# RWKV attention and a routed expert layer in one kernel: ranks one turn later, halved first products, own rows of three units on GpSimd

## The chip, the cores and the metric

The kernel runs on one core of one Trainium2 chip. A core has five engines with queues of their own: TensorE (PE in the profile, with its weight loads shown apart as PEld), VectorE (DVE), ScalarE (ACT), GpSimd (POOL) and SyncE (SP), which here issues the transfers. [...] The metric is the device time of one launch in microseconds (us), the median of several runs; lower is better. All data are float32.

## The reference

Two layers follow each other. The first is a linear attention with decay, per batch (4), head (8) and step (768), with heads of 48 channels:

```python
for t in range(S):
    kt, vt, rt = (k[:, :, t], v[:, :, t], r[:, :, t])
    cur = np.einsum('bhd,bhe->bhde', u[None] * kt, vt)
    y[:, :, t] = np.einsum('bhd,bhde->bhe', rt, state + cur)
    state = w[None, :, :, None] * state + np.einsum('bhd,bhe->bhde', kt, vt)
```

Its output, turned to 3072 tokens of 384 channels, goes into a router with eight experts. Each token is sent to the expert whose embedding has the largest cosine with it:

```python
logits = xn @ en.T / tau            # xn, en: rows divided by their norms
expert_idx = np.argmax(logits, axis=1)
...                                 # probs: softmax of logits, gate_w: its value at expert_idx
for e in range(E):
    mask = expert_idx == e
    h = np.maximum(x[mask] @ w1[e], 0.0)
    out[mask] = gate_w[mask, None] * (h @ w2[e])
```

## The kernel before

The sequence is cut into 6 chunks of 128 steps, and with 4 batches this makes 24 units; unit i is chunk i // 4 of batch i % 4. Four units of one chunk are a group. Within a chunk the recurrence is written as matrix products: K and R are turned (transposed) and scaled by powers of the decay w, scores are formed and masked, and what the state of earlier chunks contributes is added. The step's own term, which u weighs, is computed apart: `diag` is the sum over channels of K, u and R, and `xd` (the own rows) is V times `diag`.

The decays' powers and unit 0 are prepared like this:

```python
    def busy(columns):
        ps = k.ps.tile([128, 512], F32, name="wake", tag="y")
        nc.tensor.matmul(ps[:, 0:columns], k.ones, wide[:, 0:columns], start=True, stop=True)

    for _ in range(WAKE):
        busy(512)
# ...
    t = pool.tile([128, NP, C], F32, name="wpow")
    for p in range(NP):
        nc.vector.tensor_tensor_scan(
            t[:, p, :], wc[:, p : p + 1].to_broadcast([128, C]), k.ones, 1.0, ALU.mult, ALU.mult
        )
    mid = pool.tile([128, NP], F32, name="mid")
    nc.vector.reciprocal(mid, t[:, :, C // 2])
    kp = k.work.tile([128, NP, C], F32, name="kp", tag="AT0")
    nc.vector.tensor_mul(kp, t[:, :, ::-1], mid[:, :, None].to_broadcast([128, NP, C]))
    k.rpow = pool.tile([128, NP, C], F32, name="rpow")
    for p in range(NP):
        nc.scalar.mul(k.rpow[:, p, :], t[:, p, :], mid[:, p : p + 1])

    kt = turned_k(k, 0)
    k.KT[0] = k.work.tile([128, NP, C], F32, name="KT", tag="KT")
    nc.vector.tensor_mul(k.KT[0], kt, kp)
    turn_r(k, 0)
    ps = k.ps.tile([128, NP, 2, DP], F32, name="kpT", tag="xp")
    for p in range(NP):
        nc.tensor.transpose(ps[:, p].rearrange("q s d -> q (s d)"), kp[:, p, :], k.ident)
    busy(192)
    k.kpow = pool.tile([128, H, D], F32, name="kpow")
    nc.scalar.copy(k.kpow.rearrange("q (p s) d -> q p s d", s=2), ps[:, :, :, 0:D])
    cast(k)
    first = k.Kpad[0].rearrange("q (p s) d -> q p s d", s=2)[:, :, :, 0:D]
    nc.vector.tensor_mul(first, first, ps[:, :, :, 0:D])
```

Own rows exist in two forms, one on ScalarE with four scalings for each half of the heads, one as a single product on GpSimd, which only the last unit uses:

```python
def own_rows(k, i, half):
    if half == 0:
        k.xd[i] = k.work.tile([128, H, D], F32, name="xd", tag="xd")
    diag, V = k.diag[i], k.loaded[i][2]
    for h in range(half * H // 2, (half + 1) * H // 2):
        k.nc.scalar.mul(k.xd[i][:, h, :], V[:, h, :], diag[:, h : h + 1])


def own_rows_once(k, i):
    k.xd[i] = k.work.tile([128, H, D], F32, name="xd", tag="xd")
    k.nc.gpsimd.tensor_mul(k.xd[i], k.loaded[i][2], k.diag[i][:, :, None].to_broadcast([128, H, D]))
```

Each unit's R and K are turned on TensorE into a PSUM tile. The tags name PSUM banks: "tp" has two banks that are used in turn, and `rt`, `yrows`, `lgT` and `rank` all take them; "st" has one.

```python
def turn_r(k, i):

    nc = k.nc
    R = k.loaded[i][1]
    rt = k.ps.tile([128, NP, C], F32, name="rt", tag="tp")
    for p in range(NP):
        nc.tensor.transpose(rt[:, p, :], pair(R, p), k.ident)
    k.RT[i] = k.work.tile([128, NP, C], F32, name="RT", tag="RT")
    nc.vector.tensor_mul(k.RT[i], rt, k.rpow)
# ...
HELD = {"tp": (0, 1), "at": (2, 3), "y": (4, 5), "st": (6,), "xp": (7,), "ps": (0, 1, 6, 7, 2, 3, 4, 5)}
```

The rows of a unit are turned back and added to the own rows; squares are summed for the norms; the rank of each token within its expert comes from two small products, and its place is read from them:

```python
def rows(k, i):
    # ...
    y = k.ps.tile([128, 2, NP // 2, 2 * DP], F32, name="yrows", tag="tp")
    # ... four transposes of yT
    nc.vector.tensor_add(
        by_bank(X), y.rearrange("t s q (u d) -> t s (q u) d", d=DP)[:, :, :, 0:D], by_bank(k.xd.pop(i))
    )

def squares(k, g, b):
    sq = k.work.tile([128, DM], F32, name="sq", tag="sq")
    k.nc.scalar.activation(sq, g.X[:, b, :], ACT.Square, accum_out=g.ssq[:, b : b + 1])


def ranks(k, g):

    mm = k.nc.tensor.matmul
    g.rank = k.ps.tile([128, E, B], F32, name="rank", tag="tp")
    mm(g.rank, k.umask, g.oh, start=True, stop=False)
    mm(g.rank, k.ones, g.pre, start=False, stop=True)


def places(k, g):
    nc, p = k.nc, k.rt
    at = p.tile([128, E, B], F32, name="at", tag="at")
    nc.vector.tensor_mul(at, g.rank, g.oh)
    with nc.allow_low_precision(reason="whole numbers, one of each sum's terms not zero"):
        nc.vector.reduce_sum(k.pos[:, g.c, :], at.rearrange("p e b -> p b e"), axis=AX.X)
```

The loop over the units, one turn for each, gives the order in which every engine gets its instructions. `on` calls a step for one unit, `of_group` for a unit's rows, `whole` for a group when its last unit is reached. The steps that matter here, in their order:

```python
SQUARES = {1: (), 2: (), 3: (), 4: (0, 1), 5: (2, 4), 6: (3, 5)}
# ...
for i in range(-1, units):
    # ... load(k, i + AHEAD)
    whole(places, i - 4)
    whole(logits_out, i - 3)
    if i >= 0:
        on(turn_r, i + 1)
    # ...
    if B <= i < units - 1:
        on(own_rows, i, 0)
    if i >= 0:
        on(turn_k, i + 1)
    # ...
    on(scaled, i + 2)          # Kpad: K times powers, GpSimd
    on(own, i + 2)             # KU: K times u, then times R, GpSimd
    for n in SQUARES.get(i, (i - 1,)):
        of_group(squares, n)
    if B <= i < units - 1:
        on(own_rows, i, 1)
    # ... choose and before (VectorE)
    whole(located, i - 4)
    # ... gates, lanes, listed
    on(own_sum, i + 1)         # diag, VectorE
    on(sums, i)                # y: state part, then scores times V; ScalarE copies it to yT
    on(states, i)
    # ... carry
    on(scores, i + 1)
    on(masked, i + 1, 0)
    on(rows, i)
    on(masked, i + 1, 1)
    # ... of_group(put, i)
    of_group(turn_rows, i - 1) # xp
    whole(logits, i - 2)
    whole(ranks, i - 3)
    # ...
    if 3 <= i < 3 + len(k.ring):
        k.nc.gpsimd.memset(k.ring[i - 3], 0.0)
```

After the loop two experts get an early tile, then all eight run, each as products of its tokens with its two weight matrices, and rows are written to their tokens by indirect transfers.

Of the kernel before, what the change touches and what calls it, by code (L numbers as in the profile page):

```python
# [10 lines left out]
F32 = mybir.dt.float32  # L11
I32 = mybir.dt.int32
ACT = mybir.ActivationFunctionType
ALU = mybir.AluOpType
# [3 lines left out]
B, H, S, D = 4, 8, 768, 48  # L18
DM, E, F = H * D, 8, 1024
N = B * S  # L20
C = 128
NCH = S // C
DP = 64
NP = H // 2
# [14 lines left out]
TG = TT // TM  # L39
WAKE = 2  # L40
AHEAD = 5
SQUARES = {1: (), 2: (), 3: (), 4: (0, 1), 5: (2, 4), 6: (3, 5)}


class Net:
# [3 lines left out]
def build_first(k):  # L49


    nc, pool = k.nc, k.aconst
    wc = pool.tile([128, NP], F32, name="wc")
    nc.vector.memset(wc, 1.0)
    with nc.allow_non_contiguous_dma(reason="384 words"):
        for s, q in ((0, nc.sync), (1, nc.scalar)):
            q.dma_start(out=wc[s * DP : s * DP + D, :], in_=k.w.rearrange("(p s) d -> s d p", s=2)[s])
    k.ones = k.const.tile([128, 128], F32, name="ones")
    nc.vector.memset(k.ones, 1.0)
    wide = k.work.tile([128, 512], F32, name="wide", tag="AT1")  # L60
    nc.vector.memset(wide, 1.0)
    k.ident = k.const.tile([128, 128], F32, name="ident")
    make_identity(nc, k.ident)

    def busy(columns):
        ps = k.ps.tile([128, 512], F32, name="wake", tag="y")
        nc.tensor.matmul(ps[:, 0:columns], k.ones, wide[:, 0:columns], start=True, stop=True)

    for _ in range(WAKE):
        busy(512)  # L70
    k.Kpad, k.Rpad = (
        [pool.tile([128, H, DP], F32, name=f"{name}{i}") for i in range(count)]
        for name, count in (("Kpad", 4), ("Rpad", AHEAD + 2))
    )
    pads = k.Kpad + k.Rpad
    for t in pads:
        nc.gpsimd.memset(t[:, :, D:DP], 0.0)
    load(k, 0, k.Kpad[0])
    for i in range(1, AHEAD - 1):
        load(k, i)  # L80
    load_rows(k)


    nc.gpsimd.tensor_scalar(wc, wc, W_MIN, W_MAX, ALU.max, ALU.min)
    build_numbers(k)
    own_k(k, 0)
    t = pool.tile([128, NP, C], F32, name="wpow")
    for p in range(NP):
        nc.vector.tensor_tensor_scan(
            t[:, p, :], wc[:, p : p + 1].to_broadcast([128, C]), k.ones, 1.0, ALU.mult, ALU.mult  # L90
        )
    mid = pool.tile([128, NP], F32, name="mid")
    nc.vector.reciprocal(mid, t[:, :, C // 2])
    kp = k.work.tile([128, NP, C], F32, name="kp", tag="AT0")
    nc.vector.tensor_mul(kp, t[:, :, ::-1], mid[:, :, None].to_broadcast([128, NP, C]))
    k.rpow = pool.tile([128, NP, C], F32, name="rpow")
    for p in range(NP):
        nc.scalar.mul(k.rpow[:, p, :], t[:, p, :], mid[:, p : p + 1])

    kt = turned_k(k, 0)  # L100
    k.KT[0] = k.work.tile([128, NP, C], F32, name="KT", tag="KT")
    nc.vector.tensor_mul(k.KT[0], kt, kp)
    turn_r(k, 0)
    ps = k.ps.tile([128, NP, 2, DP], F32, name="kpT", tag="xp")
    for p in range(NP):
        nc.tensor.transpose(ps[:, p].rearrange("q s d -> q (s d)"), kp[:, p, :], k.ident)
    busy(192)
    k.kpow = pool.tile([128, H, D], F32, name="kpow")
    nc.scalar.copy(k.kpow.rearrange("q (p s) d -> q p s d", s=2), ps[:, :, :, 0:D])
    cast(k)  # L110
    first = k.Kpad[0].rearrange("q (p s) d -> q p s d", s=2)[:, :, :, 0:D]
    nc.vector.tensor_mul(first, first, ps[:, :, :, 0:D])
    k.wC = t[:, :, C - 1 : C].to_broadcast([128, NP, D])
# [16 lines left out]
def load_rows(k):  # L130
    nc = k.nc
    k.emb_rows = k.aconst.tile([E, DM], F32, name="emb")
    nc.sync.dma_start(out=k.emb_rows, in_=k.emb)
    k.tau_rows = k.aconst.tile([E, 1], F32, name="tau")
    nc.sync.dma_start(
        out=k.tau_rows, in_=bass.AP(tensor=k.tau.tensor, offset=k.tau.offset, ap=[[0, E], [1, 1]])
    )
    k.wrow = k.const.tile([1, DM], F32, name="wrow")
    nc.sync.dma_start(out=k.wrow, in_=k.w.rearrange("(o h) d -> o (h d)", o=1))
# [172 lines left out]
def pair(t, p):  # L312
    return t[:, 2 * p : 2 * p + 2, :].rearrange("q h d -> q (h d)")
# [35 lines left out]
def own_rows_once(k, i):  # L349
    k.xd[i] = k.work.tile([128, H, D], F32, name="xd", tag="xd")  # L350
    k.nc.gpsimd.tensor_mul(k.xd[i], k.loaded[i][2], k.diag[i][:, :, None].to_broadcast([128, H, D]))


def turn_r(k, i):

    nc = k.nc
    R = k.loaded[i][1]
    rt = k.ps.tile([128, NP, C], F32, name="rt", tag="tp")
    for p in range(NP):
        nc.tensor.transpose(rt[:, p, :], pair(R, p), k.ident)  # L360
    k.RT[i] = k.work.tile([128, NP, C], F32, name="RT", tag="RT")
    nc.vector.tensor_mul(k.RT[i], rt, k.rpow)  # L362


def turned_k(k, i):
    Kw = k.Kpad[i % len(k.Kpad)]
    kt = k.ps.tile([128, NP, C], F32, name="kt", tag="st")
    for p in range(NP):
        k.nc.tensor.transpose(kt[:, p, :], pair(Kw, p), k.ident)  # L369
    return kt  # L370
# [476 lines left out]
def attention(k):  # L847


    units = B * NCH  # L850

    def on(f, i, *more):
        if 0 <= i < units:
            f(k, i, *more)
# [5 lines left out]
    def whole(f, i, *more):  # L860
        if 0 <= i < units and i % B == B - 1:
            f(k, k.groups[i // B], *more)

    emb, tables = build_experts(k), build_turned(k)
    for i in range(-1, units):
        j = i - SETTLED * B
        if 0 < i + AHEAD < units:
            load(k, i + AHEAD)
        whole(places, i - 4)
        whole(logits_out, i - 3)  # L870
        if i >= 0:
            on(turn_r, i + 1)
        if i == 0:
            own_sum(k, i)
        if B <= i < units - 1:
            on(own_rows, i, 0)
        if i >= 0:
            on(turn_k, i + 1)
        if 0 < i < B:
            own_rows(k, i, 0)  # L880
        whole(turn_logits, i - 3)
        if i == B + 3:
            norms(k, k.groups[0])
        on(scaled, i + 2)
        if i < 0:
            own_r(k, 0)
        on(own, i + 2)
        for n in SQUARES.get(i, (i - 1,)):
            of_group(squares, n)
        if B <= i < units - 1:  # L890
            on(own_rows, i, 1)
        if i > B + 1:
            whole(norms, i - 2)
        if j == 10:
            k.lists = turned_lists(k, perm, "tp")
            lists = taken_by_rank(k, k.lists)
            first = [Early(k, r, *lists, w) for r, w in zip(LAST, k.weights)]
        whole(choose, i - 3)
        whole(before, i - 3)
        whole(located, i - 4)  # L900
        whole(gates, i - 5)
        whole(lanes, i - 5)
        whole(listed, i - 5)
        if 0 <= i < units - 2:
            on(own_sum, i + 1)
        if j == 7:
            load_, count = loads(k, "xp")
        if j == 9:
            expert_of(k, by)
            number = expert_number(k, LAST[0])  # L910
            load_w1(k, number, k.weights[0][0])
        on(sums, i)
        on(states, i)
        for n in (0, 1) if i == 0 else (1,) if 0 < i < B else ():
            own_rows(k, i, n)
        whole(taken, i - 6, "xp")
        whole(exps, i - 4)
        on(carry, i)
        if 0 < i < B + 2:
            next(tables)  # L920
        whole(summed, i - 6)
        if i == B:
            next(emb)
        on(scores, i + 1)
        on(masked, i + 1, 0)
        if i == 0:
            masked(k, i + 1, 1)
        if i == units - 1:
            first[0].turn()
        on(rows, i)  # L930
        if i != 0:
            on(masked, i + 1, 1)
        if i == units - 2:
            own_sum(k, i + 1)
            own_rows_once(k, i + 1)
        of_group(put, i)
        if j == 10:
            load_w2(k, number, k.weights[0][1])
        of_group(turn_rows, i - 1)
        whole(logits, i - 2)  # L940
        whole(ranks, i - 3)
        if i == 0:
            build_constants(k)
        if i in (1, 2, 3):
            next(emb)
        if 3 <= i < 3 + len(k.ring):
            k.nc.gpsimd.memset(k.ring[i - 3], 0.0)
        if j == 8:
            by = order(k, load_)
        if j == 9:  # L950
            settle(k, by, count)
            perm = turner(k, by)
# [29 lines left out]
    load_, _ = loads(k, "xp")  # L982
# [635 lines left out]
```

## Time and profile before

| what | value |
|---|---|
| time, median of 3 runs | 398.76 us (398.46 to 399.27) |
| span of the profiled execution | 396.4 us |
| attention | 0 to about 130 us |
| experts (from the first transposes of gathered rows of the first full block) | 157.5 to 396.4 us |
| ScalarE own-row scalings | 184 of 324 ns (median) |
| VectorE powers of the decay | 4 scans of 128 steps, 3.69 to 5.11 us |

The profile is one execution, recorded by the hardware. Its page gives each engine's busy time, then the span in 40 slices of 9.9 us with the busy share in tenths, then the chain of work that ended last. Rows of instructions give start and duration in us, engine, line of the kernel, operation, the tiles written and read, their shapes, and in brackets the idle time of the engine before them with what ended it. A matmul of float32 appears as several records, and matmuls are pipelined, so the rows of PE overlap; the weight loads (PEld) show gaps more plainly. A wait for several semaphores is put down to the one that came last by the profile, which is not always the right name.

### The profile page before, as it was taken

Reading aid. Unit: us, or ns where it says so; the run is one execution under the profiler, and the core shown is the slowest. Engines: PE = TensorE matmul, PEld = TensorE weight load, DVE = VectorE, ACT = ScalarE, POOL = GpSimd, SP = SyncE. Lnnn points to the kernel's source line nnn. Section 1 sums busy time; section 2 is a strip of 40 time slices with the busy share of each in tenths; the row PEclk is TensorE's granted clock in tenths of the full one; section 3 lists DMA queues with packets and bytes.
Section 4 is the critical chain, followed back from the end, with each engine's and each line's share of the span. In section 5 each row is a group of like instructions: output and inputs, shape, how many; then the busy total and the mean of one; then the engine's idle time right before and its main releaser. Section 6 shows DMA issues by size and latency. Waiting matters only on the chain.

```text
span 396.4 us, 9266 instructions
## 1 busy us (share of the span) xinstructions
PE 386.9 (98%) x3542; PEld 352.5 (89%) x3542; DVE 253.2 (64%) x600; ACT 173.1 (44%) x524; POOL 160.9 (41%) x216
## 2 busy tenths in 40 slices
PE   7999999999999999999999999999999999999993
PEld 4988888889888877899999999999999999799783
DVE  6887878787788670757667668257275456655601
ACT  4887777777677412333333332233323243133120
POOL 7998796858664232500701502220350350200111
PEclk9999999999999999999999999999999999999998
DMA  7899887767606972244705532434164170150111
GB/s 146 163 215 214 189 180 162 157 136 149 142 33 206 288 285 65 87 161 163 255 7 215 196 106 94 133 112 161 55 227 159 43 237 3 40 180 0 41 39 44
DMA packets 93797, 54.35 MB, mean 137 GB/s; under 512 B 76938, under 2 KB 88381, under 8 KB 93747
## 3 DMA queue, kind: packets, MB, share of 16 engines
q1 hardware_dynamic: 90242, 44.26, 41.4%
q0 software_dynamic: 3296, 9.44, 7.3%
q8 instruction: 29, 0.48, 0.5%
q14 instruction: 22, 0.17, 0.1%
q10 hardware_dynamic: 208, 0.00, 0.0%
HBM read 44.45 MB, written 9.63 MB: 136 GB/s over the span
## 4 chain that ended last, share of the span: by engine, by line
PE 86%; SPq 4%; ACT 3%; DMA 2%; DVE 2%; POOL 1%; issue 1%; POOLq 0%; DVEq 0%; ACTq 0%
PE ps L1226 25%; PE ps L1290 18%; PE ps L1330 5%; PE at L388 4%; PE ps L1344 4%; PE y L452 4%; PE early_h L1036 3%; PE early_y L1045 3%; PE ps L1204 3%; PE yrows L470 2%; PE ps L1174 2%; PE y L443 2%; PE rt L360 2%; PE kt L369 2%; PE xp L556 2%; PE st L409 2%
## 5 line engine op out<-in xcount | busy, mean ns | idle before, releaser
L1090 POOL DMA_INDIRECT out_dram<-y,to x25 | 30.1, 1204 | 173.5 <-DVE Sh L1365 109.9
L1226 PE MATMUL ps<-xTe,w 128*128 128x192 f32 (+3 forms) x336 | 62.9, 327 | 0.0
L1226 PEld LDWEIGHTS ps<-xTe,w 128*128 128x128 f32 x336 | 55.9, 190 | 0.5
L346 ACT ACTIVATE xd<-V,diag 128x48 f32<-128x48 f32 x184 | 46.2, 326 | 0.1
L394 DVE TENSOR_TENSOR AT<-at,umask 128x512 f32<-128x512 f32 x48 | 32.7, 685 | 10.5 <-PE at L388 10.3
L1233 ACT ACTIVATE hT<-hT 128x384 f32<-128x384 f32 (+3 forms) x42 | 22.0, 523 | 32.4 <-DVE hT L1256 19.7
L1290 PE MATMUL ps<-Tw,Sh 128*128 128x192 f32 x192 | 32.5, 326 | 0.0
L1290 PEld LDWEIGHTS ps<-Tw,Sh 128*128 128x128 f32 x192 | 31.4, 190 | 0.0
L1081 POOL DMA_INDIRECT G<-xs,take x25 | 27.0, 1080 | 10.5 <-issue 4.6
L1226 PE MATMUL ps<-Tx,Sw 128*128 128x192 f32 (+3 forms) x168 | 29.7, 326 | 0.0
L388 PE MATMUL at<-RT,KT 48*128 48x128 f32 x384 | 27.9, 285 | 0.3 <-DVE RT L362 0.3
L1243 DVE TENSOR_TENSOR u<-ps,p 128x384 f32<-128x384 f32 (+3 forms) x14 | 7.8, 558 | 31.3 <-ACT p L1240 16.6
L1226 PEld LDWEIGHTS ps<-Tx,Sw 128*128 128x128 f32 x168 | 27.6, 190 | 0.1
L452 PE MATMUL y<-AT,V 128*48 128x128 f32 (+1 forms) x384 | 26.0, 278 | 0.0
L388 PEld LDWEIGHTS at<-RT,KT 48*128 48x128 f32 x384 | 23.3, 187 | 2.6 <-issue 0.7
L332 POOL TENSOR_TENSOR KU<-KU,Rpad 128x384 f32<-128x384 f32 x24 | 24.1, 1004 | 1.8
L452 PEld LDWEIGHTS y<-AT,V 128*48 128x48 f32 (+1 forms) x384 | 19.9, 124 | 4.2 <-issue 3.6
L1290 PE MATMUL ps<-w,hT 128*128 128x192 f32 x128 | 23.4, 326 | 0.0
L328 POOL TENSOR_TENSOR KU<-K,u_bc 128x384 f32<-128x384 f32 x23 | 23.2, 1008 | 0.0
L317 POOL TENSOR_TENSOR Kpad<-K,kpow 128x384 f32<-128x384 f32 x23 | 23.1, 1004 | 0.1
L558 ACT COPY xT<-xp 128x384 f32<-128x384 f32 x24 | 11.5, 479 | 25.5 <-PE xp L556 25.5
L1253 ACT ACTIVATE hT<-ps 128x384 f32<-128x384 f32 (+3 forms) x14 | 6.9, 490 | 35.7 <-PE ps L1226 35.7
(240 smaller groups left out, 816.5 us busy)
## 6 DMA issues: line engine op xcount, KB each, us to landing
w<-in_moe_w_dram SPq DMA_DIRECT2D x16, 1536.0 KB, 6.9
Rpad<-in_r_dram SPq DMA_DIRECT2D x24, 192.0 KB, 4.4
V<-in_v_dram SPq DMA_DIRECT2D x24, 192.0 KB, 4.2
xs<-X SPq DMA_DIRECT2D x24, 192.0 KB, 2.7
K<-in_k_dram SPq DMA_DIRECT2D x23, 192.0 KB, 3.7
G<-xs,take POOLq DMA_INDIRECT x27, 3.2
out_dram<-y,to POOLq DMA_INDIRECT x25, 3.5
Kpad<-in_k_dram SPq DMA_DIRECT2D x1, 192.0 KB, 3.2
```

Of the source, the lines that this page charges most:

```text
L317: k.nc.gpsimd.tensor_mul(k.Kpad[i % len(k.Kpad)][:, :, 0:D], k.loaded[i][0], k.kpow)
L328: k.nc.gpsimd.tensor_mul(k.KU[i], k.loaded[i][0], k.u_bc)
L332: k.nc.gpsimd.tensor_mul(k.KU[i], k.KU[i], k.loaded[i][1][:, :, 0:D])
L346: k.nc.scalar.mul(k.xd[i][:, h, :], V[:, h, :], diag[:, h : h + 1])
L388: nc.tensor.matmul(at[s][:, p, :], KT[rows, p, :], RT[rows, p, :], start=True, stop=True)
L394: k.nc.vector.tensor_mul(a, k.at[i][s], k.umask[:, None, :].to_broadcast([128, NP, C]))
L452: mm(y[s][u * DP : u * DP + n, q, :], V[:, h * D : h * D + n], AT[s][:, p, :], start=(c == 0 and q == 0), stop=True, skip_group_check=True,)
L1081: nc.gpsimd.indirect_dma_start(out=G[0:n, :], out_offset=None, in_=k.xs[:, :], in_offset=IndirectOffsetOnAxis(ap=take[0:n], axis=0), bound ...
L1090: put = k.nc.gpsimd.indirect_dma_start(out=k.out[:, :], out_offset=IndirectOffsetOnAxis(ap=to, axis=0), in_=y, in_offset=None, bounds_chec ...
L1226: nc.tensor.matmul(ps[:, j, :], weights[:, (f + j) * 128 : (f + j + 1) * 128], moving, start=(first and j == 0), stop=True, skip_group_che ...
L1233: nc.scalar.activation(h, h, ACT.Relu)
L1290: nc.tensor.matmul(ps, a[:, f, :], b[:, f, :], start=(first and f == 0), stop=(f == NF // 2 - 1), skip_group_check=True)
```

## The change

The change has four parts, all in the attention.

1. Ranks a turn later. The two rank products leave the end of turn i, where they stood between the transposes of X and those of the next R, and go to the next turn, behind the transposes of K and ahead of `sums`. `places` and `located` follow them there. The aim is to take a PSUM bank of "tp" at a moment when it is free.
2. The first unit's K and R scaled by halves, in turn, so that the first scores can begin when the first half of both is there. A filler matmul of 192 columns goes.
3. The decays' powers by scans of 64 steps and one product for the upper half, so that the serial scans are shorter.
4. The own rows of units 4, 5 and 20 (`ONCE`) as one product on GpSimd instead of eight scalings on ScalarE; the squares of the first units are spread anew; the clears of the gather buffers on GpSimd move from turns 3 to 10 to turns 6 to 13. The aim is to relieve ScalarE where it has most to do.

```diff
-SQUARES = {1: (), 2: (), 3: (), 4: (0, 1), 5: (2, 4), 6: (3, 5)}
+SQUARES = {1: (), 2: (), 3: (), 4: (0, 1), 5: (2, 3, 4)}
+ONCE = B, B + 1, B * (NCH - 1)
... (build_first)
+    half = C // 2
     for p in range(NP):
         nc.vector.tensor_tensor_scan(
-            t[:, p, :], wc[:, p : p + 1].to_broadcast([128, C]), k.ones, 1.0, ALU.mult, ALU.mult
+            t[:, p, 0:half], wc[:, p : p + 1].to_broadcast([128, half]), k.ones[:, 0:half], 1.0, ALU.mult, ALU.mult
         )
+    nc.vector.tensor_mul(t[:, :, half:C], t[:, :, 0:half], t[:, :, half - 1 : half].to_broadcast([128, NP, half]))
...
-    kt = turned_k(k, 0)
-    k.KT[0] = k.work.tile([128, NP, C], F32, name="KT", tag="KT")
-    nc.vector.tensor_mul(k.KT[0], kt, kp)
-    turn_r(k, 0)
+    kt, rt = turned_k(k, 0), turned_r(k, 0)
+    k.KT[0], k.RT[0] = (k.work.tile([128, NP, C], F32, name=name, tag=name) for name in ("KT", "RT"))
+    for p in (slice(0, NP // 2), slice(NP // 2, NP)):
+        nc.vector.tensor_mul(k.KT[0][:, p], kt[:, p], kp[:, p])
+        nc.vector.tensor_mul(k.RT[0][:, p], rt[:, p], k.rpow[:, p])
...
-    busy(192)
... (turn_r is split: turned_r makes the transposes, turn_r adds the scaling)
... (attention)
-        whole(places, i - 4)
         whole(logits_out, i - 3)
+        if i in ONCE:
+            own_rows_once(k, i)
         if i >= 0:
             on(turn_r, i + 1)
...
-        if B <= i < units - 1:
+        if B <= i < units - 1 and i not in ONCE:
             on(own_rows, i, 0)
... (the same for the second half)
-        whole(located, i - 4)
...
         if 0 <= i < units - 2:
             on(own_sum, i + 1)
+        for step in (ranks, places, located):
+            whole(step, i - 4)
...
-        whole(ranks, i - 3)
...
-        if 3 <= i < 3 + len(k.ring):
-            k.nc.gpsimd.memset(k.ring[i - 3], 0.0)
+        if B + 2 <= i < B + 2 + len(k.ring):
+            k.nc.gpsimd.memset(k.ring[i - B - 2], 0.0)
```

More of the change, by code (lines that the diff above doesn't have):

```diff
@@ L63, in build_first @@
     make_identity(nc, k.ident)
-    def busy(columns):
+    for _ in range(WAKE):
         ps = k.ps.tile([128, 512], F32, name="wake", tag="y")
-        nc.tensor.matmul(ps[:, 0:columns], k.ones, wide[:, 0:columns], start=True, stop=True)
-    for _ in range(WAKE):
-        busy(512)
+        nc.tensor.matmul(ps, k.ones, wide, start=True, stop=True)
     k.Kpad, k.Rpad = (
@@ L351, in own_rows_once, with turned_r @@
     k.nc.gpsimd.tensor_mul(k.xd[i], k.loaded[i][2], k.diag[i][:, :, None].to_broadcast([128, H, D]))
-def turn_r(k, i):
-    nc = k.nc
+def turned_r(k, i):
     R = k.loaded[i][1]
@@ L359, in turn_r @@
     for p in range(NP):
-        nc.tensor.transpose(rt[:, p, :], pair(R, p), k.ident)
+        k.nc.tensor.transpose(rt[:, p, :], pair(R, p), k.ident)
+    return rt
+def turn_r(k, i):
+    rt = turned_r(k, i)
     k.RT[i] = k.work.tile([128, NP, C], F32, name="RT", tag="RT")
-    nc.vector.tensor_mul(k.RT[i], rt, k.rpow)
+    k.nc.vector.tensor_mul(k.RT[i], rt, k.rpow)
 def turned_k(k, i):
@@ L889, in attention @@
             of_group(squares, n)
-        if B <= i < units - 1:
+        if B <= i < units - 1 and i not in ONCE:
             on(own_rows, i, 1)
```

## The prediction

> **What bounds the kernel now.** I read the page's busy times and slices first, then the chain that ended last, then the waits of TensorE, and then TensorE's weight loads turn by turn. A turn is one pass of the attention loop; turn i handles unit i (chunk i // 4, batch i % 4), 24 in all.
>
> ```profile
> PE 386.9 (98%) x3542; PEld 352.5 (89%) x3542; DVE 253.2 (64%) x600; ACT 173.1 (44%) x524; POOL 160.9 (41%) x216
> ...
> PEld 4988888889888877899999999999999999799783
> ...
> ACT  4887777777677412333333332233323243133120
> ```
>
> TensorE (PE) is the bound, and the row to trust is the weight loads (PEld): they show gaps where the pipelined matmuls look continuous. In the first 13 slices (0 to about 129 us, attention) they stand at 80%, later near 90%. The chain says the same: from about 36 us to the end it is PE almost throughout. So off-path work saved is worth nothing; what counts is each moment when PE waits. The change touches attention alone, so I looked for PE's waits there.
>
> Next, busy time per turn. The stretches run from one turn's transposes of y (`yrows`) to the next's; after the span come PE, PEld, DVE, ACT, POOL:
>
> ```profile
> 24.94:30.49 5.55, 5.41 (x84) 4.53 (x82) 4.84 (x10) 5.11 (x20) 5.39 (x8) 1.00 1.08 221
> 30.49:35.63 5.14, 5.01 (x80) 4.37 (x80) 3.43 (x9) 4.31 (x17) 4.89 (x8) 1.00 0.89 209
> 41.62:47.09 5.47, 5.45 (x85) 4.83 (x83) 4.99 (x13) 4.12 (x15) 4.58 (x7) 1.00 1.05 232
> 47.09:51.95 4.86, 4.86 (x81) 4.35 (x79) 4.68 (x11) 3.80 (x14) 3.95 (x6) 1.00 0.80 179
> 111.97:116.52 4.55, 4.49 (x65) 3.77 (x63) 4.33 (x11) 3.58 (x14) 3.37 (x5) 1.00 0.14 47
> ```
>
> The fourth row is a plain turn without a wait: 4.86 us. The first two (turns 4 and 5), the third (which holds a group's ranks) and the last (turn 20, which has no state matmuls) are longer than their matmuls need. Inside turn 4 (start, duration; in brackets the idle time before, and who ended it):
>
> ```profile
> 28.31 0.54 PEld L409 LDWEIGHTS st<-V,Kpad 128*64 128x64 f32 x16 [0.21 <-ACT KT L378]
> 28.91 0.26 PEld L252 LDWEIGHTS ps<-ident,emb 8*128 8x128 f32 x3
> 29.19 0.97 PEld L388 LDWEIGHTS at<-RT,KT 48*128 48x128 f32 x16
> 30.49 0.47 PEld L470 LDWEIGHTS yrows<-ident,yT 112*128 112x128 f32 x4 [0.33 <-ACT yT L457]
> ```
>
> PE waits twice for ScalarE (ACT), whose queue holds eight scalings of own rows (`xd`) and two squares in this turn. Around the ranks:
>
> ```profile
> 42.28 0.30 PEld L625 LDWEIGHTS rank<-seq,umask 128*128 128x128 f32 x2
> 42.51 0.30 PEld L626 LDWEIGHTS rank<-run,ones 128*128 128x128 f32 x2
> 42.94 0.42 PEld L360 LDWEIGHTS rt<-ident,Rpad 128*128 128x128 f32 x4
> ```
>
> ```profile
> 42.33 0.56 DVE L476 TENSOR_TENSOR X<-yrows,xd 128x384 f32<-128x384 f32 x1
> ```
>
> `yrows`, `rank` and `rt` alternate over two PSUM banks, so `rt` takes the bank of `yrows` again and needs the add that reads it: that ends at 42.33 + 0.56 = 42.89, and `rt` starts at 42.94. Last, the start:
>
> ```profile
> 7.49 0.97 PEld L388 LDWEIGHTS at<-RT,KT 48*128 48x128 f32 x16 [0.60 <-DVE RT L362]
> 8.79 0.42 PEld L360 LDWEIGHTS rt<-ident,Rpad 128*128 128x128 f32 x4 [0.33 <-POOL Kpad L317]
> ```
>
> ```profile
> L298 SPq DMA_DIRECT2D Rpad<-in_r_dram x1: 800/800/800, 3.7 to 3.7; - x1
> ...
> DMA to landing us min/median/max: 5.0/5.0/5.0
> ```
>
> The first scores wait for RT, but the next instruction waits again: unit 1's R was issued at 3.72 and landed 5.0 later, at 8.72. The name printed (Kpad) also ends at 8.72, but `rt` does not read it.
>
> **What the Trainium skill says.** "Perfetto Trace Analysis", section "Identifying the Most-Contended Engine": judge TensorE by LDWEIGHTS busy share, not by matmul occupancy. The trace agrees: turn 4 shows 5.41 of 5.55 us of matmuls, though the weight loads idle 0.54 us in the two gaps above. "PSUM — Partial Sum Buffer", section "PSUM bank collisions raise a hardware error": guard PSUM by bank and quadrant, not by address; hence the wait of `rt`, seen at 42.89 to 42.94. "GPSIMD Engine Reference", section "3.1 Elementwise — side-by-side cycle accounting": about 2.6 cycles of 1.2 GHz an element for two inputs, which for 384 elements gives an estimate of 0.83 us; the one such product in this trace (`xd` of unit 23) took 0.822, and `Kpad` beside a busy VectorE 1.00. The same page, section "1. Specifications": its SBUF interfaces are shared with VectorE. The trace fits: a 128x4 tensor_scalar took 0.70 us at 44.34, in the middle of GpSimd's products, and 0.15 right after.
>
> **The change, part by part.**
>
> Own rows of units 4, 5 and 20 on GpSimd, and squares at (0,1), (2,3,4), then one a turn. An `xd` scaling costs ACT about 0.25 us in sequence (four took 1.01), so each of these turns loses 2.0 us of ACT work; turn 5 gains one square (0.5), turn 6 loses one.
> - Turn 4: 5.55 us. A plain turn plus the embedding's transposes (28.91 to 29.19, 0.28) would be 4.86 + 0.28 = 5.14. I take 0.4.
> - Turn 5: 5.14 against 4.86, with a 0.31 wait for yT: 0.28.
> - Turn 6: it has the logits like turn 10 (57.35 to 63.27 in the chain, 5.92) and took 5.99: 0.07.
> - Turn 20: PEld waits 0.25 for yT, and `yrows` then takes 0.07 longer than unhindered: 0.3.
> Sum 1.05.
>
> GpSimd must carry this. In turn 4 it is busy 5.39 of 5.55; it drops a 0.42 clear of a gather buffer and takes a 0.82 to 1.0 product, in turn 5 again: it falls behind by about 0.5 us a turn, and the turns get shorter. But its work is needed late: `Kpad` of unit 6 ended at 28.86 and PE reads it at 31.67; `xd` of unit 4 should end by 28.5 and is read after `yrows`, near 30. No new wait. The clears move to turns 6 to 13.
>
> Ranks a turn later, behind `kt`. The two matmuls and their two DVE operations stay; the bank wait goes, because the add on `yrows` has two more transposes' time. What they cost there: the single count matmul `cp` stands in that very place in turn 19, and makes that rank turn 5.60 instead of 5.47, so 0.13; the second rank matmul follows 0.22 after the first. So 0.35, and a rank turn goes from 5.47 to 5.21: 0.26 saved. It occurs in turns 7, 11, 15 and 19 (turn 23 has no `rt`, and the order of PE's instructions is unchanged there): 4 × 0.26 = 1.05. The DVE work moves behind `RT` and `diag`, inside slack of about 1 us.
>
> The start. Four scans of 128 took 1.42 us; of 64 I estimate 0.85 plus 0.35 for the product, so 0.2 less. KT and RT come in halves in turn (about 0.33 each where the whole took 0.61), so the first scores could begin near 6.85 instead of 7.49 and end near 8.1. Then `rt` of unit 1 still waits for its R at 8.72, and `kt` for `Kpad` at 8.72. From 8.79 on PE runs without long gaps to turn 4, so nothing is left: 0. Dropping the 192-column filler matmul also gives 0, because PE idles 0.3 us behind it.
>
> After attention, PE runs the experts, and the early gather (issued at 125.6, landed 130.65, PE waiting 0.43) hangs on the same loop, so it moves with it. Sum: 1.05 + 1.05 + 0 = 2.1, and 0.1 for restarts behind removed waits: 2.2 of 398.76 leaves about 396.5 us.
>
> **The rivals.**
> 1. The start counts: if scores 0.6 us earlier survive, 395.9. For it: PE does wait for RT. Against: R lands at 8.72, and the DMA queue issues without a break until 23 us, deaf to PE.
> 2. GpSimd becomes the bound of turns 4 to 6: its busy share there is the highest of any engine but PE, and it stalls VectorE's tensor_scalars (one took 1.66 at 24.36). Then ACT's waits return as waits for `Kpad` or `diag`, and 1 us is lost: 397.5.
> 3. The ranks cost as much in their new place. At the end of the loop, where no bank is awaited, they take 128.12 to 128.69 = 0.57 of PE; if that holds, a turn saves 0.1 and the sum is 1.5: 397.3.
> 4. The gain is given back at the early gather or the first weights (issued 121.77, landed 9.9 later, needed at 132.4: 0.7 of slack). Against: both are released by the same loop. At worst 398.5.
>
> **Range and chances.** Rivals 2 and 3 together leave about 398; the start with everything else gives 395.5. The three runs before spread over 0.8 us. I take 395.2 to 398.3. 2% is 8 us, more than all of PE's gaps in attention that the change reaches, and nothing added is on the path: 0.97 for within 2%.
>
> **What would show it.** Right: `rt` of unit 1 still at about 8.8; turn 4 near 5.1, turn 5 near 4.9, no PEld wait for yT in turns 4, 5 and 20; rank turns near 5.2, with `rank` behind `kt`; the expert phase as long as before and about 2 us earlier. Wrong: PEld waits for `Kpad`, `diag` or X in turns 4 to 8; rank turns at 5.4; a wait at `early_x` that grows beyond 0.43 by what the loop saved.

## The result and the profile after

The changed kernel takes 397.21 us (median of 6 runs, 397.12 to 397.52) against 398.50 for the kernel before beside it (6 runs, 398.26 to 399.27): ratio 0.9966, 95% interval 0.9953 to 0.9979. That is 1.3 us less, where 2.2 were forecast. The span of the profiled execution fell from 396.4 to 395.0 us.

The page after, with busy times, the slices of the weight loads and of ScalarE, and the shares of the chain that ended last:

```profile
PE 385.5 (98%) x3540; PEld 352.5 (89%) x3540; DVE 255.8 (65%) x603; ACT 167.8 (42%) x500; POOL 163.8 (41%) x219
...
PEld 4998989888888777899999999999999999799783
...
ACT  4876777777666412332333332233323233133120
...
PE 93%; DMA 3%; DVE 1%; SPq 1%; POOL 0%; issue 0%; POOLq 0%; DVEq 0%
```

ScalarE lost 5.3 us of work and the weight loads lost none (352.5 in both), but they now stand in a shorter attention. The chain is TensorE for 93%. Before, its shares were these:

```profile
PE 86%; SPq 4%; ACT 3%; DMA 2%; DVE 2%; POOL 1%; issue 1%; POOLq 0%; DVEq 0%; ACTq 0%
```

ScalarE, which had 3% of it, is gone.

Busy time by turn, in the columns of the prediction's table (stretch, then the span, PE, PEld, DVE, ACT, POOL, clock, DMA share, GB/s). These are turns 4, 5, 7, 8 and 20 of the changed kernel:

```profile
24.94:30.08 5.14, 5.14 (x84) 4.61 (x82) 5.00 (x8) 3.60 (x12) 5.06 (x6) 1.00 1.11 235
30.08:34.95 4.87, 4.87 (x81) 4.35 (x79) 3.48 (x10) 3.12 (x10) 4.71 (x7) 1.00 0.70 149
40.87:46.10 5.23, 5.23 (x85) 4.85 (x83) 4.99 (x13) 4.00 (x15) 4.82 (x6) 1.00 1.06 222
46.10:50.97 4.87, 4.87 (x81) 4.35 (x79) 4.72 (x11) 3.83 (x15) 3.85 (x6) 1.00 0.88 206
110.33:114.75 4.42, 4.42 (x65) 3.77 (x63) 4.25 (x9) 2.32 (x6) 3.68 (x4) 1.00 0.14 50
```

Turn 4 fell from 5.55 to 5.14 us, turn 5 from 5.14 to 4.87, the rank turn from 5.47 to 5.23, turn 20 from 4.55 to 4.42; the plain turn 8 is unchanged. In each, PE's busy time now equals the span.

Weight loads of turn 4 in the changed kernel (start, duration, and idle time in brackets where there is any):

```profile
28.07 0.60 PEld L417 LDWEIGHTS st<-V,Kpad 128*64 128x64 f32 x16
28.72 0.26 PEld L256 LDWEIGHTS ps<-ident,emb 8*128 8x128 f32 x3
28.99 0.97 PEld L396 LDWEIGHTS at<-RT,KT 48*128 48x128 f32 x16
30.08 0.39 PEld L478 LDWEIGHTS yrows<-ident,yT 112*128 112x128 f32 x4
```

Both waits for ScalarE are gone. The same view around the ranks in turn 7:

```profile
41.97 0.47 PEld L377 LDWEIGHTS kt<-ident,Kpad 128*128 128x128 f32 x4
42.41 0.30 PEld L633 LDWEIGHTS rank<-seq,umask 128*128 128x128 f32 x2
42.63 0.30 PEld L634 LDWEIGHTS rank<-run,ones 128*128 128x128 f32 x2
42.97 0.41 PEld L451 LDWEIGHTS y<-RT,state 48*64 48x64 f32 x16
```

`rank` stands behind `kt`, and nothing waits for a bank. The start, in the same view:

```profile
7.11 1.19 PEld L396 LDWEIGHTS at<-RT,KT 48*128 48x128 f32 x16 [0.39 <-DVE RT L108]
8.79 0.42 PEld L362 LDWEIGHTS rt<-ident,Rpad 128*128 128x128 f32 x4 [0.50 <-POOL Kpad L321]
```

The first scores begin 0.38 earlier (7.11 against 7.49), but `rt` of unit 1 starts at 8.79 as before.

Added up, the changed kernel is 1.68 us ahead at the transposes of unit 22 (125.78 against 127.46), yet only 1.15 at those of unit 23 (129.89 against 131.04): 0.53 is given back in one turn. TensorE's weight loads of the early tiles show where; before:

```profile
130.76 0.31 PEld L1025 LDWEIGHTS early_x<-ident,G 128*128 128x128 f32 x3 [0.66 <-PE y L452]
```

and after:

```profile
129.61 0.31 PEld L1034 LDWEIGHTS early_x<-ident,G 128*128 128x128 f32 x3 [1.19 <-PE y L460]
```

The wait at `early_x` grew by 1.19 - 0.66 = 0.53. (The 0.43 of the prediction is the same wait in the rows of the matmuls; there it is 0.97 now.) The matmul named had long been done; what it waits for is G, the gathered rows. The gather of the first early tile, before (start of its issue, then the time to its landing):

```profile
L1014 POOL DMA_INDIRECT G<-xs,take x1: 1323/1323/1323, 125.6 to 125.6; - x1
...
DMA to landing us min/median/max: 5.1/5.1/5.1
```

and after:

```profile
L1023 POOL DMA_INDIRECT G<-xs,take x1: 1323/1323/1323, 123.9 to 123.9; - x1
...
DMA to landing us min/median/max: 5.6/5.6/5.6
```

It was issued 1.7 us earlier, with the loop, but took 0.5 longer. Ahead of it in the transfers is the load of the first expert's weights (1.5 MB). It is issued once `who`, that expert's number, is known, and `who` was only 1.14 earlier (119.40 against 120.54). The reason stands in VectorE's rows of turn 20. Before:

```profile
115.12 0.66 DVE L679 TENSOR_TENSOR lane<-lanes,place 128x512 f32<-128x512 f32 x1
...
118.36 0.47 DVE L754 TENSOR_TENSOR more<-load 128x64 f32<-128x64 f32 x1
```

After:

```profile
113.22 1.42 DVE L687 TENSOR_TENSOR lane<-lanes,place 128x512 f32<-128x512 f32 x1
...
116.89 0.80 DVE L762 TENSOR_TENSOR more<-load 128x64 f32<-128x64 f32 x1
```

The same comparison of two SBUF tiles takes 0.76 more. GpSimd's last product of that turn before:

```profile
113.95 1.00 POOL L332 TENSOR_TENSOR KU<-KU,Rpad 128x384 f32<-128x384 f32 x1
```

and its rows of the same stretch after:

```profile
110.27 0.83 POOL L355 TENSOR_TENSOR xd<-V,diag 128x384 f32<-128x384 f32 x1
111.06 1.00 POOL L321 TENSOR_TENSOR Kpad<-K,kpow 128x384 f32<-128x384 f32 x1
112.01 1.01 POOL L332 TENSOR_TENSOR KU<-K,u_bc 128x384 f32<-128x384 f32 x1
113.10 0.99 POOL L336 TENSOR_TENSOR KU<-KU,Rpad 128x384 f32<-128x384 f32 x1
```

The new first product pushes the last one to 113.10 to 114.09, onto `lane`. Before, that last product ended at 114.95 and `lane` began at 115.12, while GpSimd stood idle until 116.06. "GPSIMD Engine Reference", section "1. Specifications", of the Trainium skill says that VectorE instructions with two SBUF inputs contend with GpSimd for SBUF; these rows fit it, and the experiments test it.

**Theory.** The two expected gains, ScalarE's waits in turns 4 to 6 and the bank wait at the ranks, are real. Unit 20's product on GpSimd costs more than it brings: it slows `lane` and `more`, so `who` and the first weights come late, and the gather, whose landing follows that load, holds up TensorE. **Rival A:** the gather's landing hangs on its own issue alone, and the 0.5 is chance. **Rival B:** ranks in their new place slow VectorE's path to `who`. **Rival C:** the start brings or costs something that the turns hide.

### The profile page after: what moved, and what is told of

Read it like the earlier page. It is cut to its first block, busy times and chain, and to the rows that moved or that the text cites. A ratio compares the mean times of both kernels' runs of the same rounds, so it can differ in the third digit from the quotient of the medians.

```text
span 395.0 us, 9252 instructions
## 1 busy us (share of the span) xinstructions
PE 385.5 (98%) x3540; PEld 352.5 (89%) x3540; DVE 255.8 (65%) x603; ACT 167.8 (42%) x500; POOL 163.8 (41%) x219
## 4 chain that ended last, share of the span: by engine, by line
PE 93%; DMA 3%; DVE 1%; SPq 1%; POOL 0%; issue 0%; POOLq 0%; DVEq 0%
PE ps L1235 25%; PE ps L1299 18%; PE at L396 6%; PE y L460 6%; PE ps L1339 5%; PE ps L1353 4%; PE yrows L478 3%; PE early_h L1045 3%; PE early_y L1054 3%; PE y L451 3%; PE rt L362 3%; PE ps L1213 3%; PE ps L1183 2%; PE kt L377 2%; PE st L417 2%; PE xp L564 2%
## 5 line engine op out<-in xcount | busy, mean ns | idle before, releaser
L350 ACT ACTIVATE xd<-V,diag 128x48 f32<-128x48 f32 x160 | 40.2, 326 | 0.0
```

## The experiments

Each ratio is against the kernel before, timed beside it. Times of two kernels from different groups are compared through their ratios.

**The change in its parts.** Three kernels carry one part each, and a fourth is the changed kernel without unit 20's product. The ranks alone:

```diff
+        for step in (ranks, places, located):     # behind own_sum
+            whole(step, i - 4)
-        whole(ranks, i - 3)                       # and places, located from their old lines
```

> The kernel before with the ranks' move alone. My theory: turns 7, 11 and 15 lose 0.24 us each and turn 19 loses 0.16, in all 0.88; VectorE is not stalled in turn 20, so the first weight load and the early gather move by the same 0.9 and nothing is given back: about 0.9 us less than the kernel before. Rival (any gain of the loop is given back at the early gather, whatever its source): 0.3 us or less, with a wait at early_x near 1.5 us.

Measured 398.11 us against 399.18: ratio 0.9975 (0.9966 to 0.9985), 1.07 less. `lane` took 0.66, the wait at `early_x` is 0.71, and turns 7, 11, 15 and 19 fell by 0.24, 0.25, 0.25 and 0.17. All of it reaches the end, and rival B falls.

The start alone (halves, scans of 64 steps, no filler):

```diff
+    for p in (slice(0, NP // 2), slice(NP // 2, NP)):
+        nc.vector.tensor_mul(k.KT[0][:, p], kt[:, p], kp[:, p])
+        nc.vector.tensor_mul(k.RT[0][:, p], rt[:, p], k.rpow[:, p])
```

> The kernel before with the halved first products and the shorter scans alone. My theory: the first scores end about 0.2 us earlier but the R of unit 1 still lands at 8.7 us, so the time is that of the kernel before within 0.15 us and the first yrows stays at 12.38. Rival (the start carries through): 0.3 to 0.6 us less.

Measured 399.10 against 399.18: ratio 0.9998 (0.9990 to 1.0006). Rival C falls, in either direction beyond about 0.4 us.

The own rows alone (three units on GpSimd, squares and clears moved):

```diff
-SQUARES = {1: (), 2: (), 3: (), 4: (0, 1), 5: (2, 4), 6: (3, 5)}
+SQUARES = {1: (), 2: (), 3: (), 4: (0, 1), 5: (2, 3, 4)}
+ONCE = B, B + 1, B * (NCH - 1)
```

> The kernel before with the own rows of units 4, 5 and 20 on GpSimd, the squares and the clears moved, alone. My theory: turns 4 to 6 gain 0.75 us, but the GpSimd product in turn 20 stalls VectorE (the lane comparison takes 1.4 us instead of 0.66), the first weight load is issued only about 0.25 us earlier, the early gather lands about 2.4 us behind that load, and so the time is only 0.2 to 0.4 us less than before. Rival (the gather's landing hangs on its own issue, not on the load): 0.75 us less.

Measured 398.97: ratio 0.9993 (0.9984 to 1.0001), 0.21 less, not surely different from nothing. Its `lane` takes 1.42 and `more` 0.79, the wait at `early_x` is 1.12. So the giving back belongs to this part.

The changed kernel with two units on GpSimd:

```diff
-ONCE = B, B + 1, B * (NCH - 1)
+ONCE = B, B + 1
```

> The changed kernel with unit 20's own rows back on ScalarE. My theory: TensorE waits for yT in turn 20 again (0.3 us lost there), but VectorE's lane comparison is back at 0.66 us, the first weight load is issued 0.5 us earlier than in the changed kernel, the gather lands at about 129.0 us instead of 129.5, and the time is about 396.85, 0.35 less than the changed kernel. Rival (the own rows of unit 20 save what they save in their turn): 397.4 or more.

Measured 397.59: ratio 0.9960 (0.9946 to 0.9973), 1.59 less. The changed kernel's own ratio is 0.9966 here and 0.9967 in the repetition below, so the totals lean the expected way, about 0.25 us, with overlapping intervals. The trace is plainer. VectorE's row of `lane`:

```profile
114.50 0.66 DVE L687 TENSOR_TENSOR lane<-lanes,place 128x512 f32<-128x512 f32 x1
```

and TensorE's at the early tile:

```profile
130.16 0.31 PEld L1034 LDWEIGHTS early_x<-ident,G 128*128 128x128 f32 x3 [0.69 <-PE y L460]
```

`lane` and the wait are back at the old kernel's 0.66 and about 0.7; in exchange turn 20 is 4.55 again, with a 0.25 wait for yT. What unit 20's product costs in all can be read from the `yrows` of unit 19 to the first products of the early tile, `early_h`: 20.34 us before, 20.35 with the ranks only and 20.34 with two units, but 20.73, 20.68 and 20.65 in the changed kernel, its repetition (below) and the own rows alone. So it loses 0.3 to 0.4 us, its gain in turn 20 included.

**Load and gather.** The changed kernel was run again unaltered, as the neighbour of the next three:

> The changed kernel unaltered, as the yardstick on the chip of its neighbours: 1.3 us less than the kernel before.

Measured 398.13 against 399.42: ratio 0.9967 (0.9955 to 0.9980), with `lane` at 1.42, a gather of 5.5 us and a wait of 1.14. It repeats the result. In its profile unit 0's `yrows` stand 0.7 later, turns 1 and 3 are 0.1 longer, and turn 4 is 5.35 instead of 5.14; the reason for turn 4 is a VectorE row:

```profile
25.45 1.65 DVE L210 TENSOR_SCALAR mask<-number,own 128x8 f32<-128x8 f32 x1
27.01 0.68 DVE L402 TENSOR_TENSOR AT<-at,umask 128x512 f32<-128x512 f32 x1
```

A small tensor_scalar of the embedding takes 1.65 us beside GpSimd's products. In the profile of the result it does so too, but it began 0.69 ahead of turn 4 (24.25 against 24.94), early enough. Here it began only 0.39 ahead of it, holds AT up, and TensorE waits 0.26 for AT in that turn.

Next, the first weight load was put behind the store of unit 22's rows, so that the gather meets no load:

```diff
-            load_w1(k, number, k.weights[0][0])     # in turn 21, ahead of sums
+            load_w1(k, number, k.weights[0][0])     # in turn 22, ahead of the second weights
```

> The changed kernel with the first weight load issued only behind the store of unit 22's rows, so that it does not run beside the early gather. My theory (the gather is held up by that load): it lands 3.5 us or less after its issue instead of 5.6, and TensorE starts the early transposes without a wait; the late load then costs more than that, about 2 us. Rival (the gather takes its 5 us by itself): it still lands 5 us or more after its issue.

Measured 403.9 us in a single run, at a mean granted clock of 0.989 (0.995 to 0.999 in the other profiles), so the total is rough. The gather:

```profile
L1023 POOL DMA_INDIRECT G<-xs,take x1: 1318/1318/1318, 125.0 to 125.0; - x1
...
DMA to landing us min/median/max: 3.4/3.4/3.4
```

and the early tile's weight loads:

```profile
129.72 0.31 PEld L1034 LDWEIGHTS early_x<-ident,G 128*128 128x128 f32 x3 [0.18 <-issue]
...
135.73 1.36 PEld L1045 LDWEIGHTS early_h<-earlyx,w 128*128 128x128 f32 x6 [3.95 <-DMA w<-in_moe_w_dram]
```

Rival A falls: issued at the same point of the turn (9.17 us behind unit 20's transposes in both), the gather took 3.4 instead of 5.5 us, and `early_x` no longer waits. But the weights themselves now come 3.95 too late, which I had put at 2. The load must be early.

So the expert's number and its load were moved from within turn 21 to the end of turn 20, with three units and with two:

```diff
         if j == 8:                                  # turn 20; the same lines leave j == 9
             by = order(k, load_)
+            expert_of(k, by)
+            number = expert_number(k, LAST[0])
+            load_w1(k, number, k.weights[0][0])
```

> The changed kernel with the first expert's number and its weight load right behind the ordering of the experts, at the end of turn 20 instead of within turn 21. My theory: the load is issued about 0.8 us earlier, the gather lands as much earlier, 2.3 us behind the load, while the scores of unit 22 wait about 0.5 us more for RT; about 0.6 us less than the changed kernel. Rival (the gather's landing hangs on its own issue): no gain, or 0.5 us more.

> The same early weight load, with the own rows of units 4 and 5 alone on GpSimd. My theory: the load is issued near 119.3 us of the first chip's clock, the gather lands near 128.2, TensorE does not wait at early_x, and the time is 2.1 us less than the kernel before, 0.8 less than the changed kernel. Rival: 1.6 us less than the kernel before, as without the early load.

Measured 399.10, ratio 0.9992 (0.9984 to 1.0001), and 398.60, ratio 0.9977 (0.9968 to 0.9985). Neither is faster than the kernel it was made from: the first is slower than the changed kernel, the second stands above the one with two units by 0.0017 of ratio, with intervals that just overlap. This forecast missed. The gather did land 3.9 us after its issue and `early_x` did not wait. But the two-input comparison `eq` has moved beside a GpSimd product as well; with two units, VectorE:

```profile
118.26 0.22 DVE L766 TENSOR_REDUCE by<-more 128x8 f32<-128x64 f32 x1
118.51 0.79 DVE L789 TENSOR_TENSOR eq<-by,number 1x64 f32<-1x64 f32 x1
```

GpSimd:

```profile
118.22 1.00 POOL L336 TENSOR_TENSOR KU<-KU,Rpad 128x384 f32<-128x384 f32 x1
```

It takes 0.79 where it took 0.20, on a single partition. All this stands ahead of RT, so the scores of the next unit wait: turn 21 takes 5.70 us with two units and 6.32 with three, against 4.93 and 5.03.

The traces together, with times behind the start of unit 20's `yrows`:

| kernel | `lane` us | load issued | gather issued | gather took | gather lands behind load's issue | `early_x` |
|---|---|---|---|---|---|---|
| before | 0.66 | 5.25 | 9.08 | 5.1 | 8.9 | 14.24 |
| ranks only | 0.66 | 5.25 | 9.09 | 5.1 | 8.9 | 14.30 |
| two units | 0.66 | 5.24 | 9.07 | 5.1 | 8.9 | 14.26 |
| changed | 1.42 | 5.88 | 9.17 | 5.6 | 8.9 | 14.86 |
| changed, again | 1.42 | 5.87 | 9.16 | 5.5 | 8.8 | 14.80 |
| own rows only | 1.42 | 5.87 | 9.16 | 5.5 | 8.8 | 14.78 |
| number early, two | 0.66 | 4.89 | 9.85 | 3.9 | 8.9 | 14.53 |
| number early, three | 1.42 | 5.50 | 10.46 | 3.9 | 8.9 | 15.15 |
| load late | 1.42 | 12.85 | 9.17 | 3.4 | none ahead | 13.85 |

In the eight rows where the load is ahead, the gather lands 8.8 to 8.9 us behind the issue of the load, whether it was itself issued 3.3 or 5.0 us after it. That is how a load released 0.63 late makes a gather issued 0.09 late land 0.6 late. "DMA: Bandwidth & Descriptors", section "Issuing engines are not separate DMA queues", of the Trainium skill says that transfers started by ScalarE, SyncE or GpSimd all run on the same 16 DMA engines and interleave; the 3.4 against 5.5 us agrees.

**Towards a better version.** In the changed kernel the list of slots (`settle`) stands ahead of the turning of the order (`turner`), and TensorE waits 0.33 for it in turn 22. The order of the two was swapped:

```diff
+            perm = turner(k, by)
             settle(k, by, count)
-            perm = turner(k, by)
```

> The changed kernel with the permutation of the lists worked out ahead of the settling of the last experts, which frees the early gather to be issued about 0.4 us earlier and takes away TensorE's 0.33 us wait ahead of the lists product. My theory (the gather's landing hangs on the first weight load): the gather still lands 2.2 to 2.4 us behind that load, TensorE's wait at early_x grows by what was saved, and the time is that of the changed kernel within 0.15 us. Rival (the landing hangs on the gather's own issue): 0.35 us less.

Measured 398.44 against 399.97: ratio 0.9959 (0.9946 to 0.9973). The 0.33 is gone, but the wait at `early_x` grew from 1.14 to 1.50, and `early_x` starts 14.81 behind unit 20's `yrows`, as in the repetition (14.80). The ratio lies within the changed kernel's interval. It agrees with the theory, a wait ahead of the gather only moves; but the gather's issue came no more than 0.08 earlier, so as a test it is inconclusive.

Then order, number and load were all moved up into turn 19, with three units, with two, and with three and the swap:

```diff
-        if j == 8:
-            by = order(k, load_)
+            by = order(k, load_)                    # at j == 7, behind loads(...)
+            expert_of(k, by)
+            number = expert_number(k, LAST[0])
+            load_w1(k, number, k.weights[0][0])
```

> The changed kernel with the ordering of the experts, the first one's number and its weight load in turn 19, right behind the loads from which they are worked out. VectorE has about 1 us of idle time there, and turns 20 and 21 lose 1.3 us of its work. My theory: the load lands before the early gather is issued, the gather lands within 3.9 us of its issue, TensorE waits neither for RT in turn 21 (0.3) nor at early_x (1.1): 1.2 us less than the changed kernel, 2.5 less than the kernel before. Rival (the gather or VectorE in turn 19 gives it back): no better than the changed kernel.

> The same with the own rows of units 4 and 5 alone on GpSimd. My theory: with VectorE unburdened in turns 20 and 21 the product of unit 20 no longer harms, so this one is 0.15 to 0.3 us slower than its neighbour, because TensorE waits for yT in turn 20; 2.2 us less than the kernel before. Rival (the product of unit 20 harms by itself): faster than its neighbour.

> The ordering in turn 19 and the permutation ahead of the settling, together, with three units on GpSimd. My theory: now that the gather is free of the load, the 0.33 us ahead of the lists product is a real gain: 2.8 us less than the kernel before, 1.5 less than the changed kernel. Rival: as without the permutation's move.

Measured 398.11, 398.13 and 397.85 us against 399.97: ratios 0.9954 (0.9941 to 0.9968), 0.9955 (0.9941 to 0.9968) and 0.9944 (0.9930 to 0.9958). In all three the first `early_x` no longer waits for the gather. The last has the lowest ratio of all versions tried: 2.12 us below the kernel before. It lies about 0.0022 of ratio below the changed kernel, and their intervals overlap slightly; so no version is surely faster than the changed kernel. All three gained less than forecast.

The second of them also settles what slows `lane`. It has only two units on GpSimd, but `lane` takes 1.47:

```profile
114.26 1.47 DVE L687 TENSOR_TENSOR lane<-lanes,place 128x512 f32<-128x512 f32 x1
```

beside GpSimd's

```profile
114.17 1.01 POOL L336 TENSOR_TENSOR KU<-KU,Rpad 128x384 f32<-128x384 f32 x1
```

The reason is that `order` and `who` now stand in turn 19, ahead of VectorE's `state`, for which GpSimd's products wait. GpSimd's first row of the stretch with two units and the number in its old place, then here:

```profile
110.81 0.51 POOL L433 TENSOR_TENSOR state<-state,wpow 112x192 f32<-112x192 f32 x1 [1.80 <-DVE state L432]
```

```profile
111.64 0.52 POOL L433 TENSOR_TENSOR state<-state,wpow 112x192 f32<-112x192 f32 x1 [2.60 <-DVE state L432]
```

Against unit 19's `yrows`, which start at 111.35 and 111.36, GpSimd is 0.82 later, and so is its last product. So it is the overlap, not unit 20's product as such. It costs nothing there: `who` is past, and turn 21 takes 4.94. With unit 20's product as well, in the first and the third, `lane` starts 0.8 later still (at 115.06 in the third), AT stands behind it, and TensorE waits in turn 21, which takes 5.18:

```profile
118.90 0.39 PEld L460 LDWEIGHTS y<-AT,V 128*48 128x48 f32 x8 [0.37 <-DVE AT L402]
```

So there too the product takes back what it brings in turn 20.

What stops the fastest version is the next wait in line. Its weight loads at the early tiles:

```profile
129.48 0.31 PEld L1032 LDWEIGHTS early_x<-ident,G 128*128 128x128 f32 x3 [0.19 <-issue]
...
131.28 0.31 PEld L1032 LDWEIGHTS early_x<-ident,G 128*128 128x128 f32 x3 [0.70 <-ACT earlyx L1034]
```

and ScalarE:

```profile
130.58 0.23 ACT L654 ACTIVATE l<-l 128x32 f32<-128x32 f32 x1 [0.56 <-DVE l L653]
130.72 0.46 ACT L1034 COPY earlyx<-early_x 128x384 f32<-128x384 f32 x1
```

The second early tile needs the bank of the first, which ScalarE copies out at 130.72 to 131.18. That copy stands in ScalarE's queue behind the exponentials, which wait for VectorE's `l`; and `l` stands behind a `tile` of 128x4 that takes 0.62 beside GpSimd's product for unit 23 (0.17 in turn 19). So freeing the gather shortens the first wait and opens this one. With two units it brings nothing: from unit 19's `yrows` to `early_h` 20.35 us pass with the number in turn 19 and 20.34 without. The third version takes 20.16. That the copy is the limit is a reading of the trace; no run moved it.

## Why the prediction was right, and where it was not

The range held, for 397.21 lies within 395.2 to 398.3, but 1.3 of the 2.2 us came, and two steps failed. By its own steps:

- **Turns 4, 5, 6** (0.4, 0.28, 0.07): 0.41, 0.27 and 0.07 in the result. Turn 4 was worth only 0.2 in the repetition, and 0.2 to 0.39 in the other runs with this part, by how far ahead of the turn `mask` began: it took 5.16 to 5.22 where that was 0.53 to 0.59 us, and 5.35 or 5.36 where it was 0.38 or 0.39. So the second rival, VectorE's tensor_scalars stalled by GpSimd, is real there and up to half as large as the gain; it does not show in the profile of the result.
- **Rank turns** (4 × 0.26 = 1.05): 0.24, 0.25, 0.25 and 0.16, in sum 0.90. The mechanism is as written. In turn 19 the count matmul `cp` stands beside the ranks, and I took the turn's gain for that of the others; next to them it costs 0.21 (5.44 against 5.23), not the 0.13 I took. The third rival, at 0.1 a turn, falls.
- **Turn 20** (0.3): 0.20, of which 0.13 in that turn and 0.07 in the next. Here I added a wait in brackets (0.25) and a longer `yrows` (0.07, which by these stretches falls into turn 21). But without the wait, 0.12 us still passes between the end of the scores' weight loads (113.66 + 0.97 = 114.63) and `yrows` (114.75), as in turn 8. A bracket holds that changeover too. For turn 4 I had compared with a plain turn, and that came out right.
- **The start** (0): 0, by the same `rt` at 8.79 and by the kernel with that part alone. The scans with their product brought 0.11 (`kp` starts at 5.25 instead of 5.36), not 0.2, and the halves of KT and RT took 0.42 each, not 0.33; so the first scores began at 7.11, not 6.85. Nothing hung on it.
- **GpSimd's extra product, "No new wait"**: this step failed. I asked when GpSimd's products are read, not what they stand beside. VectorE's RT comes late behind the slower `more` and ends at 118.54; the scores of unit 22 start at 118.66, behind a gap of 0.31 instead of 0.17. This cost turn 21 0.17; with the 0.07 of the shorter `yrows` it grew by 0.10.
- **"The early gather … hangs on the same loop, so it moves with it"**: this step failed, and it is the largest term, 0.53 at the transposes of unit 23. The gather's issue moved with the loop (1.68), its landing moved with the weight load (1.14). I also misread the load: of the fourth rival's "landed 9.9 later", the 9.9 us is that of the load issued at 129.26; the first load took 6.6, from 121.77 to 128.4, and was in flight when the gather was issued at 125.6. That rival's mechanism happened, at a quarter of its worst size.
- **Restarts** (0.1): not found as such. From unit 23's transposes to the end the kernel gained another 0.1 to 0.3 on the 1.15 (1.29 by the medians, 1.4 by the spans). Of this, 0.10 comes at once: the second `early_x` waited 0.25 for the copy of the first, and no longer does, so `early_h` starts 1.25 earlier (131.06 against 132.31).

The shortfall: 0.15 (ranks) + 0.10 (turn 20) + 0.17 (turn 21) + 0.53 (gather) = 0.95, of 2.1 expected without restarts; it leaves 1.15, the lead at unit 23. The sign named in advance, a wait at `early_x` that grows, appeared.

## What to carry to other kernels

Work handed to an engine that looks idle shifts that engine's later work, so look at what the shifted instructions will then run beside; here GpSimd's products held up VectorE's comparisons with two SBUF inputs and some of its small tensor_scalars until they ended. A small transfer issued behind a large one lands when the large one lets it: if the loop gets shorter, the release of the large one must move too. Read a wait's gain as the difference to the same place in an unhindered turn, not as the number in the bracket.

## What the runs showed of the hardware that was not expected

- A VectorE operation with two SBUF inputs that began beside a GpSimd product of 128x384 ended only behind that product. `lane` (128x512) took 1.42 instead of 0.66 us and ended 0.55 behind it (114.64 against 114.09; with the number in turn 19 again 0.55). `more` (128x64) took 0.80 and `eq` (1x64) 0.79, and both ended 0.08 behind it; with no product beside them they took 0.22 and 0.20. The 0.47 of `more` in the kernel before was such a wait already, also 0.08 behind a product's end. AT, which has a PSUM input, kept 0.68 us beside such products.
- Single-tile tensor_scalars can suffer too: `mask` (128x8) took 1.64 to 1.66 us in all 14 profiles, and each time ended 0.02 to 0.03 behind the second of two GpSimd products that followed each other without a gap. In the profile of the ranks alone `tie` (128x8) took 2.84 instead of 0.16, across four GpSimd instructions on end, which held up AT and made turn 6 0.5 us longer in that execution. The section named above counts VectorE's 2-port mode among what contends as well; whether these ran in it, no run shows.
- The gathers of an early tile took 3.1 to 5.6 us, by how much of the 1.5 MB load was still ahead.
